# One core, thresholded attention and a maxout feed-forward: the ninth key blocks of a head quad multiplied together in 64x64 tiles, and a new order of work

## The chip, the cores and the metric

The kernel runs on one core of one Trainium2 chip. The metric is the device time of one launch in microseconds (us). Five engines of the core work side by side, each through its own list of instructions in order: TensorE (PE in the profile, with its weight loads as PEld), VectorE (DVE), ScalarE (ACT), GpSimd (POOL), and SyncE (SP), which here only issues DMA transfers. They wait for each other by semaphores.

## The reference, cut to what matters

```
q, k, v: (8, 8, 576, 64) f32     tau = 0.02
scores = (q @ k^T) / 8                       per batch and head, 576 x 576
keep   = scores >= rowmax(scores) - tau      everything else becomes exp(-huge) = 0
attn   = exp(scores - rowmax) * keep;  attn /= rowsum(attn)
x      = attn @ v, heads side by side        (4608, 512)
h      = max(x @ w1, x @ w2, x @ w3)         512 -> 768
out    = h @ w_out                           768 -> 512, f32
```

## The kernel before, in words

**Quads and tiles.** Four heads of one batch make a quad; there are 16. A quad's head number is 2r + i with r and i in 0 and 1. The 576 rows of a head are nine blocks of 64 queries (and nine of 64 keys). A *tile* is 128 query rows against all 576 keys of the heads of one r; a quad has nine chunks of two tiles (r = 0 and 1), so 18 tiles, and the program has 288.

**A tile's way.** `scores` (line 287) multiplies in f32 into one of four slots of PSUM (`bank`, line 179; a slot is two banks of 512 f32 columns). DVE takes the row maximum (`maximum`, line 319). Then the tile goes one of two ways, fixed by a 0 or 1 in the string `MASKED`. Unmasked (0): ACT runs a Prelu that reads PSUM and then an Exp with a row sum. Masked (1): DVE has copied the negated scores out of PSUM together with the maximum, ACT runs one Exp, and DVE does the comparison, the product and the row sum in one instruction (`numerators`, line 339). DVE makes the reciprocals of a chunk, POOL scales both tiles to bf16 (`normalized`, line 351, the tile `P`), and SP issues a transposing DMA (`turned`, line 360) into the quad's `ptq`: nine blocks of 128 keys by 1152 columns. In blocks 0 to 3 lie the first eight key blocks of r = 0, in blocks 5 to 8 those of r = 1, and block 4 holds the ninth key blocks of both: r = 0 on partitions 0 to 63, r = 1 on 64 to 127.

**The product with V.** `product` (line 366), once per quad and r, runs over five blocks m: four with `vb` (V of 128 keys) and the fifth with `vrb`, which is V of the ninth key block padded with zeros on the other r's 64 partitions, so that all 128 rows of block 4 can be multiplied. For each m and each run of columns (512 and 64 wide) two matmuls stand side by side, i = 0 and 1, each 128 rows by 64 columns of the array. In the profile these are `o<-ptq,vb` and `o<-ptq,vr`. The padded tiles `vrs` are made once (line 219) and their zero halves set by six memsets on DVE (line 553); `cast_v` (line 221) fills them with two POOL casts per quad. One product is copied out of its slot by DVE (r = 0), the other by ACT (r = 1), into `xt`. Batch 7 alone is cut into two parts of 256 and 320 query columns, so it has four products per quad of half the width.

**The feed-forward.** `ffn` (line 432) follows a batch behind: 18 hidden pieces `ph` per batch (six column blocks by three weight matrices), of which ACT copies the first and DVE takes the maximum with the others (`hm`, `hT`), and output pieces `po`. A piece is issued in two halves (F and B in the order), each 64 rows by 128 columns of the array, two abreast.

**What sets the order.** Nothing is scheduled by the compiler: `_Ordered` chains each engine's instructions as they are written, and the string `ORDER` says in which order they are written. A letter is one step: S a tile's scores, T a transpose of q or k on PE, O a product, F and B the halves of a feed-forward piece (the digit is the PSUM slot), m the maximum, e the first pass of ACT, n the second one of an unmasked tile, k that of a masked one on DVE, r reciprocals, p one scaling on POOL, q a swap of q's halves, y a cast of V, z a weight cast, t a transposing DMA, l a load, g a weight load, o a store, w and x the copies of a product by DVE and ACT, h and v those of hidden pieces, u those of output pieces. Since each engine takes its letters in order and waits by semaphore, only the order of letters of one engine among themselves acts, and the buffers that they share.

Of the kernel before, what the change touches and what calls it, by code (L numbers as in the profile page):

```python
# [24 lines left out]
010100101001000000011101001010000001100010001000101000011000100000100000  # L25
000011111001100001001001001001000001011100101001000110001010010000010011
000010011101100001001100100001001010001100010111000001000100000110000101
001001001101100000110001000100100100001100100011100111010011010111110110
# [12 lines left out]
lllllmlyelgS2ymylS3emgnlT0mleS1lakS2nlqermS3ylmeS0pmeS1kpS3elmS2nlzmelrmnT1pS0tcnperkT1pameS1zmteS3knpS0rnmp  # L41
emS2permeqS1mnqT3meqktepS0ncS2ntrpmS3npretprmeS1pmnS0tpmS3npmS1etpmeS0rT2mnplkeT1akgeS2qmgepmteS3rkpekntS0pe
rrnmT2pncS3ptamepS1meqtrS2meyqnS3lmqeS0pmelpknT1lpS2nmeymeS3lrkepS0tcnT2rpnmS1tpnmaprrmS0eS2pmteS1pmT3epctep
meT3O0ykntnyS2etrykpnO1wnprmaS0xptrS3meS2zmeS1mzgeS0mlnS3pmleS1pmelO2qmelpkteO0nrnklpS3nlwgxprrmS2leS0pmeF3q
tmT1eBqcF0eqkthBpnS2vS1nF3pmnF0pmBerBkepS2vhT1tnprmS0S3apmetS1zmeS2rmpeF3tmF0epBkepF1tnBvBznvS2ghS3rymnF0gmS
1eplBrkepF2tnmF3BnpvBnqvT1S0hprrcT2S3pamS1eymzF2emBeqgkF0etyS3nS1vpnmtF2pBmezBveS3prgnS0mtS1phrmT3epO2metzeF
0wpnS1gcqS2nmBqnmO3zekepgS1xvlF2nS3mtnF0rrmpBeBlpveS1lphS2mntF3zmeBrpS0evS1lpnmF2lnpS3rmleBptmS1nzvS0nS3mtpn
S2rpeF1rmepmtepS0mBepmtekF3ektekT2uBarklpukS0uqlS2urS1mlnS3pmleO0pmlepmelO2wtnkS1xrS0tepmF2myF3eBkepT1tBhcF0
nqvT2T1laByrcynS3qvS2nlqmF1tnpF0meS3pBelmBlhrrF2kpelS1vnBlprF3mnlS0pveBtprmS1hS2pmeS3tpmeS0pmF2emF1eBkeT3Bva
tF0nvqT2T3BkqlaS1nrcS3phmtS2npmF0epF1mteBqkBeqF3lnvS2lnBrvplS0hmtpS1F3meS2mteBrmepS0vnpO1rekpnO3mtnpweS2yrrt  # L50
xS1mF0yymT3epBcnS1pvS2nptF3meS0pmeBomT2hS1okeF0omF3ntBkaBervS1ponrF2vpemS0ptuS3mpeF2metknT1T3rknBparrceS0puS
3mqtuS1mpeS2mpeS3lmF0peomepS1ketqT3S2ncBqnmlqnmlO3ekluktO1urnwperrS0pxS3mptnS2mS1pempS3etmF0peF2meBlkBelS1kh
oF3nrmlF0pnBtvpBerrvS2phlS1mnpS3tmF0peS2mpeBmeF3vF1eoBkntS0vnBS2rmhpS3mepS1mteyF2mF0eyBkteBnrvT3pF1aovT2ynBp
lrcS3hplS0mnyF2lmF1elBykepBlnvT3tS0aS2vnO3rrmtpnmpeS1weptS2mS0prmO3eqtmeqF1eqlT0S2xqcBnlpmS3hlpS0meF2ymF1elB
knlF3vnBokBetS2hvS0nrrF3mpF1mpeBkBpetF2vnprS0uvnT3ptmS2aS1pmeS0trmF3epmnpkeS2tS0ermpBnmopnkS1uS2rurompS0eF3o
mpelmpeS2lkpeS0lmS1elqBmelqmetkO2unktO0erwpurkpT1txT2cS3apF0nmtT1qS2ceBqmnS1yF3hmF2eyrBpeBvptnF0pS1vnBrmtpS3
hS2pmeS0mtS1eF3meF2meBkBeF0knF1vnBBrvhpS3nvT0pF2akyF1tnBmyS0velByrmlS3phS2rlempF1lmyeF0pklBepS3tnvS2nBrmptO1
meprvepS2wnS3plmF0nF1rmepBlkeqS2lBhmtT3nyS0vnS2mqlO1emtpecT2xT0rS3pacF1eqmF2lnyBklqeT0BvlaS3khoS1qnmF0tF2pme
BrBopnvS3teprvF0pnrmS1puS2meS3prmS0epF1tmepmepT2ktBeqncT3tuS0kaS2urqmS3tnpmS1nF0pmemteS3repS1mS2lepmBelykteS
3kuO1rumplnmlpO0ewterpT2xS1cqnoS3mpF0nF2metBkeBkF1hlF3nvBlnrrS0pvlnBpmS2lhS1ymleF0mtS3epBmepF2vF1etkBnS0vnS3  # L60
rmBnpS2rhmpF0emF1pteBkpBerF3vnS2ptvnT0pBramS1pthS0mepF3meqtT2rBecpS1nvylT0ynS2pmlS3amlS1eomS0elO2rmpeomeplO3
ketnwT1F0nctF2xkBnBrvpS1hrF3pmS0qBemqS2onvF1yeF0mBopkeF3tyBnS2vqhBrlrnmpT1S0vaptS2empF1S3mpelBkeplF0vntS2rum
S1pnS0mtepF3rmepmetqS2kS0epBnmmteS1rkepS2lmuS0ulpmS1nlymT3yetF2cekeT3oBrknpamoS0npS3mnS1qtmuO0qurrmqelO2wpel
kpelS0xS3meptF2mS1peBemytF0hrkT3pBecF2nS1vpnS3rymtBpnmS0epS1vlnF3mF2etBmeBkhF0lkeF3nBrvpS1nrvBpnS2mptS0hmpeS
3meF2tmF1eBkeBlrvnT0plS3ravlpS2nlmqF0nlS1mqeBtrrmpF2eS3phBlmepS0tvepS1mS2npS3mepO0meknO1meownT3orxkT2pS0tacF
1nF2qrmeBtpS3evpBmS0tyhF1meT2yBcqoeF3rpkT2F0aptBnvBnS2pvS1hqtmF3nqT0meBrS1npvF2npmT3BactS1ervF3prmS0pueS2omp
F3ekqelmT1ntS0qcnBpmekteS2S1urrmpF0uompekS3eptS2nmS1pnmlO3ermtpekO2pnwS1ykxtyS3emS2BomeyrmepS1rukpS2uoF3meF0
opmnBtykBhpS1ervS2eptmO3pO0mxnS3txS2rmepF0empF1ekBtBevF3hkS2nS0mnBrmF1npF2vepBkBtS0hvO3emO2xkS1xerS3rpmF2mpF
0eF1kpteBnBvpF3BvtBrhkpF2S0vS1prmBptmF3eF0pveBtBhS1vS2mS3mF0F1mBkBF2vhF3keBeO0vnO1kF2kxeBwurS1rvpS0mpS2F3mpe
tmpeS0eoF1mnketBknkBurrupoF2puF0hptF3uvF2pvF1hF0tvF3rvpF2hF1vopF0vF3thF2vF1vF0hoF3vF2ovF1hF0vF3vO2uoO1wF0xF3  # L70
F2hF1vF3vF2hF1vF3vF2hF1vF3vF2hF1vF3vF2hF1vF3vF2hF1vBvF3uuooBF2uuuooo
# [31 lines left out]
def kernel(  # L103
# [262 lines left out]
    def product(L, r, target, part=None):  # L366
# [19 lines left out]

        def on_vector():
            ps = st["ps"]
            dst = target(L["b"])[:, 2 * L["qd"] + r, :]
            if part is None:  # L390
                vector.tensor_copy(out=dst, in_=ps[:, 0:S])
            else:
                vector.tensor_copy(out=dst[:, 256:S], in_=ps[:, 0:320])

        def on_scalar():
# [6 lines left out]
            else:  # L402
                scalar.activation(out=dst[:, 256:S], in_=ps[:, 0:320], func=AF.Copy)
        p = _Piece((L["b"], L["qd"], r, part), first)
        p.vector = on_vector if part != 1 and r == 0 else None
        p.scalar = on_scalar if part == 1 or r == 1 else None
        return p
# [188 lines left out]
    line = {k: [] for k in "menkrptahvuxwcq"}  # L596
# [6 lines left out]
    def issue(what, where):  # L603
# [149 lines left out]
```

## Time and profile before

| | us |
|---|---|
| median of 3 runs | 447.69 (447.66 to 450.87) |
| profiled execution: span from first to last instruction | 445.0 |
| what lies around the span (median less span) | 2.7 |
| PE busy | 423.6 |
| ACT busy | 394.4 |
| DVE busy | 393.2 |
| POOL busy | 315.9 |

The profiled execution has no time of its own beside its span; the median of the runs is 2.7 us longer, and those 2.7 us are taken as what lies around the span. "Busy" is a union of spans of instructions, and a matmul's span in the profile is longer than the time for which it holds the array (their starts are closer together than their ends), so a busy PE can still have short holes; start times of neighbouring matmuls tell more.

### The profile page before, as it was taken

How to read it: one execution, taken by the hardware profiler on the slowest of the kernel's cores; microseconds unless marked ns; L12 is line 12 of the kernel's file. 1: busy time of each engine (PE TensorE's matmuls, PEld its weight loads, DVE VectorE, ACT ScalarE, POOL GpSimd, SP SyncE). 2: the span in 40 equal slices, each digit the busy share in tenths (PEclk: the TensorE clock that was granted, in tenths of full speed). 3: DMA queues.
4: the chain of work that ended last, by engine and by line, in shares of the span. 5: the costliest groups of instructions: out<-in, count | busy, mean ns of one | idle time of the engine just before them, and what ended most of it. 6: DMA issues, size and time to landing. Idle time of an engine off the chain costs nothing.

```text
span 445.0 us, 14089 instructions
## 1 busy us (share of the span) xinstructions
PE 423.6 (95%) x5193; PEld 313.3 (70%) x5193; DVE 393.2 (88%) x1093; ACT 394.4 (89%) x804; POOL 315.9 (71%) x422
## 2 busy tenths in 40 slices
PE   7767799999999999999999999999999999999995
PEld 5434557767787767777687867867687778777772
DVE  4989889999999999989989998999999999989641
ACT  4999999999999999999998999999999999956422
POOL 3998989989686686686768885859767789562300
PEclk9998899999999999999999999999999999999999
DMA  8989999999999978999797999899999979882902
GB/s 251 331 162 213 243 195 234 221 245 229 215 255 195 250 165 175 234 187 228 179 223 170 200 224 182 211 234 199 197 220 202 253 121 173 148 122 34 217 13 108
DMA packets 212773, 87.44 MB, mean 196 GB/s; under 512 B 185824, under 2 KB 199648, under 8 KB 212704
## 3 DMA queue, kind: packets, MB, share of 16 engines
q1 hardware_dynamic: 212000, 85.69, 93.6%
q10 hardware_dynamic: 704, 0.85, 0.6%
q8 instruction: 41, 0.67, 0.6%
q14 instruction: 28, 0.23, 0.2%
HBM read 34.60 MB, written 9.44 MB: 99 GB/s over the span
## 4 chain that ended last, share of the span: by engine, by line
PE 81%; ACT 7%; DVE 6%; issue 4%; POOL 2%; DMA 1%; DVEq 0%; POOLq 0%; ACTq 0%
PE ph L91 30%; PE sc L91 28%; PE po L91 11%; PE o L91 8%; ACT z L91 6%; PE tp L91 4%; DVE z L91 2%; DVE unused L91 2%; DMA qm<-in_q_dram 1%; POOL P L91 1%; DVE hm L91 0%; POOL w L91 0%; ACT qt L91 0%; POOL qs L91 0%; DVE hT L91 0%
## 5 line engine op out<-in xcount | busy, mean ns | idle before, releaser
L91 POOL TENSOR_SCALAR P<-z,rs 128x576 bf16<-128x576 f32 x288 | 228.1, 807 | 85.7 <-DVE rs L91 36.4
L91 PE MATMUL sc<-kt,qt 64*128 64x320 f32 (+2 forms) x640 | 179.1, 429 | 4.9 <-ACT z L91 4.4
L91 PE MATMUL sc<-kt,qs 64*128 64x256 f32 (+2 forms) x640 | 178.6, 418 | 4.7 <-ACT z L91 2.7
L91 PE MATMUL ph<-xt,w 64*128 64x288 bf16 (+2 forms) x2160 | 163.9, 283 | 0.3
L91 PEld LDWEIGHTS <-w 64*128 64x128 bf16 (+1 forms) x2160 | 124.8, 94 | 30.9 <-issue 5.3
L91 DVE TENSOR_SCALAR_CACHE_REDUCE unused<-sc 128x576 bf16<-128x576 f32 x183 | 133.2, 749 | 8.9 <-PE sc L91 8.4
L91 ACT ACTIVATE z<-sc,nm 128x576 f32<-128x576 f32 x183 | 131.3, 740 | 8.5 <-DVE unused L91 5.2
L91 ACT ACTIVATE z<-z 128x576 f32<-128x576 f32 x183 | 123.5, 680 | 0.1
L91 PEld LDWEIGHTS sc<-kt,qs 64*128 64x128 f32 (+1 forms) x640 | 92.4, 178 | 25.3 <-ACT z L91 8.1
L91 PEld LDWEIGHTS sc<-kt,qt 64*128 64x128 f32 (+1 forms) x640 | 92.4, 178 | 19.8 <-ACT z L91 9.3
L91 DVE SCALAR_TENSOR_TENSOR z<-z 128x576 f32<-128x576 f32 x105 | 84.1, 811 | 0.4 <-ACT z L91 0.4
L91 DVE TENSOR_SCALAR_CACHE_REDUCE z<-sc 128x576 f32<-128x576 f32 x105 | 77.7, 752 | 7.4 <-PE sc L91 3.4
L91 ACT ACTIVATE z<-z,nm 128x576 f32<-128x576 f32 x105 | 79.1, 773 | 3.6 <-DVE z L91 3.2
L91 POOL COPY qs<-qt 64x640 f32<-64x640 f32 (+3 forms) x68 | 47.0, 692 | 14.4 <-ACT qt L91 11.0
L91 PE MATMUL po<-wo,hT 64*128 64x512 bf16 (+1 forms) x480 | 54.0, 356 | 0.1
L91 DVE TENSOR_TENSOR hm<-ph,hm 128x576 bf16<-128x576 f32 (+2 forms) x54 | 37.0, 686 | 13.0 <-PE ph L91 11.8
L91 ACT ACTIVATE hm<-ph 128x576 bf16<-128x576 f32 (+2 forms) x54 | 32.1, 594 | 18.4 <-PE ph L91 18.1
L91 PEld LDWEIGHTS <-hT 64*128 64x128 bf16 (+1 forms) x480 | 29.6, 97 | 17.1 <-issue 2.9
L91 DVE TENSOR_TENSOR hT<-ph,hm 128x576 bf16<-128x576 f32 (+2 forms) x54 | 37.2, 688 | 3.1 <-PE ph L91 0.6
L91 PE MATMUL o<-ptq,vb 128*64 128x64 bf16 (+2 forms) x544 | 38.7, 282 | 0.0
L91 ACT ACTIVATION_READ_ACCUMULATOR z<-z 128x1 f32 x183 | 36.2, 198 | 0.0
L91 PEld LDWEIGHTS <-vb 128*64 128x64 bf16 x544 | 22.6, 111 | 15.1 <-issue 6.8
(32 smaller groups left out, 274.2 us busy)
## 6 DMA issues: line engine op xcount, KB each, us to landing
vm<-in_v_dram SPq DMA_DIRECT2D x32, 256.0 KB, 5.1
out_dram<-ob SPq DMA_DIRECT2D x31, 256.0 KB, 2.8
qm<-in_q_dram SPq DMA_DIRECT2D x15, 512.0 KB, 4.5
km<-in_k_dram SPq DMA_DIRECT2D x15, 512.0 KB, 5.4
stage<-in_moe_w_dram SPq DMA_DIRECT2D x9, 512.0 KB, 5.3
ptq<-P SPq DMA_TRANSPOSE x144, 4.1
stage<-in_moe_w_out_dram SPq DMA_DIRECT2D x3, 512.0 KB, 4.7
qm<-in_q_dram SPq DMA_DIRECT2D x16, 64.0 KB, 2.9
```

Source lines behind the costliest of these rows:

```text
L91: ins = fn(*a, **kw)
```

## The change

Four things change.

1. `vrb` is a tile of 128 keys by two heads and no zeros: partitions 0 to 63 hold V of the ninth key block for r = 0, partitions 64 to 127 for r = 1. One cast on POOL fills it; the three padded tiles, their memsets and the second cast go.
2. A product runs over four blocks only and leaves its sums open. A new step N, after both products of a quad (and part), issues the ninth key blocks of both: for each run of columns four matmuls of 64 rows by 64 columns, r = 0 on the upper rows of the array and r = 1 on the lower, each r into its own slot. Only then are both products copied out (w and x).
3. In the second part of batch 7 the columns of the product stand at 256 to 575 of the slot, where they stood at 0 to 319.
4. `MASKED` has 114 ones in place of 105, and `ORDER` is another string: the same steps, with 18 N more and 16 y fewer, in another order on every engine.

```
-    vrs = [one.tile([128, 4, D], BF16, name=f"vr{x}") for x in range(3)]
...
-        L["vrb"] = vrs[(2 * L["b"] + L["qd"]) % 3]
-        for r in range(2):
-            rows = slice(64 * r, 64 * r + 64)
-            pool.tensor_copy(out=L["vrb"][rows, 2 * r:2 * r + 2], in_=L["vr"][rows])
-            yield
+        L["vrb"] = vp.tile([128, 2, D], BF16, name="vrb")
+        pool.tensor_copy(out=L["vrb"], in_=L["vr"])
+        yield
...
-                2: ((256, 896, 0, 256), (512, 576, 256, 64))}[part]
-
-        order = [(m, run) for m in range(5) for run in runs] if part is None else \
-            [(m, run) for run in runs for m in range(5)]
+                2: ((256, 896, 256, 256), (512, 576, 512, 64))}[part]
+
+        order = [(m, run) for m in range(4) for run in runs] if part is None else \
+            [(m, run) for run in runs for m in range(4)]
 
         def first(where):
             st["ps"] = ps = bank("o", where)
             for m, (*q0, p0, n) in order:
                 for i in range(2):
-                    w = vb[:, 2 * r + i, (1, 3, 0, 2)[m], :] if m < 4 else vrb[:, 2 * r + i, :]
-                    tensor.matmul(ps[64 * i:64 * i + 64, p0:p0 + n], w,
-                                  pt[:, 4 if m == 4 else m + 5 * r, q0[i]:q0[i] + n],
-                                  start=(m == 0), stop=(m == 4))
+                    tensor.matmul(ps[64 * i:64 * i + 64, p0:p0 + n], vb[:, 2 * r + i, (1, 3, 0, 2)[m], :],
+                                  pt[:, m + 5 * r, q0[i]:q0[i] + n], start=(m == 0), stop=False)
+
+        def ninths(run):
+            *q0, p0, n = run
+            rows = slice(64 * r, 64 * r + 64)
+            for i in range(2):
+                tensor.matmul(st["ps"][64 * i:64 * i + 64, p0:p0 + n], vrb[rows, i, :],
+                              pt[rows, 4, q0[i]:q0[i] + n], start=False, stop=True)
...
-    for t in vrs:
-        for x in range(2):
-            vector.memset(t[64 - 64 * x:128 - 64 * x, 2 * x:2 * x + 2, :], 0.0)
...
             p.first(where)
-            for k, fn in (("x", p.scalar), ("w", p.vector)):
-                if fn:
-                    line[k].append(fn)
+            line["N"].append(p)
+        elif what == "N":
+            both = [line["N"].pop(0) for _ in range(2)]
+            for run in both[0].runs:
+                for p in both:
+                    p.ninths(run)
+            for p in both:
+                for k, fn in (("x", p.scalar), ("w", p.vector)):
+                    if fn:
+                        line[k].append(fn)
```

The order at three places. PE, quad 0 (batch 0), around its products with V. Before, the first product ends with its own ninth block (`vr`), a tile's scores follow, and then the second product begins:

```order
L91 LDWEIGHTS vr_100
L91 MATMUL o<-ptq,vr_100 64x64
L91 MATMUL sc<-kt,qt 128x256
L91 MATMUL sc<-kt,qs 128x320
L91 LDWEIGHTS vb
L91 MATMUL o<-ptq,vb 64x512
```

In the changed program PE goes at this quad from the last block of the second product straight to the ninths:

```order
L91 MATMUL o<-ptq,vb 64x64
L91 LDWEIGHTS vb
L91 MATMUL o<-ptq,vb 64x64
L91 LDWEIGHTS vrb
L91 MATMUL o<-ptq,vrb 64x512
```

and leaves them with scores:

```order
L91 LDWEIGHTS vrb
L91 MATMUL o<-ptq,vrb 64x64
L91 MATMUL sc<-kt,qt 128x320
L91 MATMUL sc<-kt,qs 128x256
L91 MATMUL sc<-kt,qt 128x256
```

What moved: the ninth blocks of both products stand behind both, eight matmuls in a row, and the scores no longer stand between the products.

PE, quad 1, from the end of its products to the first hidden piece of the feed-forward (`ph`, with the weights `w_63`). Before:

```order
L91 LDWEIGHTS vr_101
L91 MATMUL o<-ptq,vr_101 64x64
L91 MATMUL sc<-kt,qs 128x256
L91 MATMUL sc<-kt,qt 128x320
L91 MATMUL sc<-kt,qs 128x320
L91 MATMUL sc<-kt,qt 128x256 x2
L91 MATMUL sc<-kt,qs 128x320
L91 LDWEIGHTS w_63
L91 MATMUL ph<-xt,w_63 128x288
```

Now:

```order
L91 LDWEIGHTS vrb
L91 MATMUL o<-ptq,vrb 64x64
L91 MATMUL sc<-kt,qs 128x320
L91 MATMUL sc<-kt,qt 128x256
L91 LDWEIGHTS w_63
L91 MATMUL ph<-xt,w_63 128x288
```

What moved: three tiles' scores stood between the products and the first hidden piece, and one stands there now; 48 tiles' scores stood ahead of quad 1's products, and 49 do now, so the first hidden piece comes after 50 tiles in place of 51.

ACT, around its copy of quad 1's second product (`xt<-o`). Rows with `z<-sc,nm` are the first pass of unmasked tiles, `z<-z,nm` that of masked ones, `z,sm<-z` the second pass of unmasked ones. Before:

```order
L91 ACTIVATE z<-z,nm 128x576
L91 ACTIVATE z<-sc,nm 128x576 x2
L91 ACTIVATE z,sm<-z 128x576 x3
L91 ACTIVATE xt<-o 128x576
L91 ACTIVATE z<-sc,nm 128x576
```

Now:

```order
L91 ACTIVATE z<-z,nm 128x576
L91 ACTIVATE z<-sc,nm 128x576
L91 ACTIVATE z<-z,nm 128x576
L91 ACTIVATE xt<-o 128x576
L91 ACTIVATE z<-sc,nm 128x576
```

What moved: six passes of tiles stand directly ahead of the copy before, three of them second passes; now the second passes stand behind it.

More of the change, by code (lines that the diff above doesn't have):

```diff
@@ L24 @@
 MASKED = """
[L25 to L28, printed above, removed]
+001110001000100001011000011010010001001000101101001001000000100000011000
+001010100111100001001001000100010001011100101001100010001010010000111000
+110010100101010010011100000001001011000110100110111001000100001110000101
+001010001101110001100001000100100100001100001101010110110101000111111111
 """
@@ L46 @@
[L46 to L65, printed above, removed]
@@ new lines @@
+hS1S2emS0zlpgtpF3F1qemmettkeBqvBS2rnnzF0T3mtBvpnhpkS2meraeF1S0BS3mgevmF2nprS1mepypqBpnF0S3lvkBegF2F1BmhrvS0z
+tneBpplzF3nnS2mvBeS1T0mrtT2mhS3pncgpgaS2F0mtBererlmpekvS1emF3S2nntS0pBlemeS1ppzqtS2mvmrF3qentT0pBF1rcmS0pppz
+nhenBS3mvO2rmgO1NekglentexnS0F3S1klwmmrnF2plpqypeeBzpBvS0hS1tmF3S2mBtrF1pzpneemrS0vBlneS3mvnS2mrppyS0mnemF1k
+S2eS3mreptnepBepmS0F3kpmrS2uutS1kenmnT0arBpekS2emtupueS0mkptpqqO1lltO3emNrlelpkwS2tllxltrlS0F3myF1lmBnpeekph
+T2cBF0T3T2vnanqpBS1cvqmF3S2BmneF0hrS1pyperBkF3S2mnBrvmvF0enS1BtS2plmmloppeS3hS0eS1emmtpmF3eekF2BBleF0tlT1vnt
@@ new lines @@
+rBvT3aT2haS1pS0kF2crtS3nmBnpmtmF0eS1tqpeeqvBptlmrppF2nveS3lntBmrlF0hS1kpyeBS2mpnvmrenpqyplS3O1qtO0mrNepexkT2
+nS3wF0cS1mrBpmnenS2S1oF3vF0pBtmmeS1pekhlS2toF3rBmmeptynevlT1aBprS2vS0nmmeF1ukketepF3kS1mT2T0rrcBS1ptpqnnaoup
+umS0eppmrS2S3mmeeeS0F1eS2qnkpkmT3BS0rnceunrmkmueppS3tlltemO2epO1NotllltS0krwpxS3ppqyF2qnpnmS1BmeS3hF0emmeeF2
+BnS1BkrvmnrF3loS0BvpleyyrS2mnpmpphS1ppF0etmS3emllBeF1nF2BtevkrpS0BvS3nS1hmmtleS2lmmetF3tkF0eBpleT1BvrvanT2nF
+3cS1BnmF0S2BrhkF3mpeT1vnrBpprveaS0S2nmT1S3pqpncmpS0meeeqmeS1tO2pqmtotlloeO3ltqNF0S1klwBxrpkppS2mrhmF3S0epBmF
@@ new lines @@
+2nenS1pvBF0mF3nleBBtottvkS2hF0keF1rurvpmT3BeapkppyrpvS1S2mnS3S0pnemF1mtS3emkS2rpBenepltS0memkmrutpuS2neS3emF
+1rmpqkynpS2pqeBemS0uuS2O3kmemekO1NeS0rwT2xoF1olppnT3mnT0BcS2aS3rncqhF0qtF1pBtemmpBkevrF2eS3vlmpnBptnlS0S1S3h
+ermmempS2F0ypmF1BBelrteoevnF3T2F0akkqvBBS2nhkymF1pqpnF3verBBS0rvtpmhnS2S1F3mrmlpBpeS0evlmS2eF1pnS3BmnleF2mtl
+lvrlttS0eppptyBmS1ehF3lepT2BmltnS0lnltcS1rkvO2O3tmNpmeprT1nnexrapkwS0pqF3qyemT1T2cpBF0S1anepkBS2hvF3S0mreBF1
+mekmrnvF2qBeS3vS0unpS2tS1omlrmeppqptlmmnF3pktT0BpecS1eekryuT2uaS0mnS3lomtmrtleF2enpS1kpS3qppnemmS0Bmkerppeue
@@ L72 @@
+S3pmF0oeBmrBokettF2peuokoruoF3uhF1pkkF2hvvruF3pF1F2hppF0pvvF3F1vvF2F0F3hvtovhtF1F2F0F3htvF1voF2O0uvO3NvF1xwF
+2hF3F0vF2vhF3F0F2hvF3vvF0F2F3vF0hF2hovF3vF0F2vhF3vvF0vBuuF2BuouoF3uooo
 """
@@ L392, in on_vector @@
             else:
-                vector.tensor_copy(out=dst[:, 256:S], in_=ps[:, 0:320])
+                vector.tensor_copy(out=dst[:, 256:S], in_=ps[:, 256:S])
         def on_scalar():
@@ L402, in on_scalar @@
             else:
-                scalar.activation(out=dst[:, 256:S], in_=ps[:, 0:320], func=AF.Copy)
+                scalar.activation(out=dst[:, 256:S], in_=ps[:, 256:S], func=AF.Copy)
         p = _Piece((L["b"], L["qd"], r, part), first)
@@ L406, in product @@
         p.scalar = on_scalar if part == 1 or r == 1 else None
+        p.runs, p.ninths = runs, ninths
         return p
@@ L595 @@
                 O=products(), F=pieces())
-    line = {k: [] for k in "menkrptahvuxwcq"}
+    line = {k: [] for k in "menkrptahvuxwcqN"}
     casts = iter([w[1] for w in wl])
```

25 lines of the change are left out of this document (14 added, 11 removed).

## The prediction

> **What bounds the kernel now.** I read the page first, its busy times and its forty slices of 11 us.
>
> ```profile
> span 445.0 us, 14089 instructions
> PE 423.6 (95%) x5193; PEld 313.3 (70%) x5193; DVE 393.2 (88%) x1093; ACT 394.4 (89%) x804; POOL 315.9 (71%) x422
> PE   7767799999999999999999999999999999999995
> DVE  4989889999999999989989998999999999989641
> ACT  4999999999999999999998999999999999956422
> ```
>
> Four engines look full on average, so the averages decide nothing. The slices do: PE is at 7 or so in the first five and at 9 from then to the last but one, while ACT is at 9 in just those first slices. So there are two regimes, and I asked for windows cut where they change. Columns: stretch, its length, then busy us of PE, PEld, DVE, ACT, POOL with instruction counts, granted clock, DMA share, GB/s.
>
> ```profile
> 10.00:50.00 40.00, 27.11 (x229) 15.82 (x230) 37.14 (x111) 39.09 (x84) 37.88 (x49) 0.94 1.05 244
> 50.00:67.50 17.50, 16.36 (x166) 10.52 (x166) 14.79 (x44) 16.89 (x35) 14.77 (x21) 0.94 1.09 199
> 67.50:400.00 332.50, 332.01 (x4291) 252.33 (x4290) 313.41 (x865) 315.89 (x642) 252.98 (x333) 1.00 1.01 203
> 430.00:445.00 15.00, 10.53 (x90) 5.98 (x87) 4.36 (x9) 3.57 (x8) 0.00 (x0) 0.99 0.21 80
> ```
>
> From 10 to 50 us ACT is busy 39.09 of 40 and PE 27.11: the start is paced by ACT, with POOL (37.88) and DVE (37.14) just behind. There is no feed-forward work yet, because batch 0 must pass through attention first. From 67.5 to 400 PE is busy 332.01 of 332.5, ACT 315.89 and DVE 313.41: PE bounds this stretch, with 16.6 us (5.0%) left on ACT and 19.1 (5.7%) on DVE. So PE time saved after 67.5 shortens the program nearly in full as long as ACT and DVE stay below PE, and the start gets shorter only by what ACT sheds.
>
> The boundary is the first hidden piece, from the timeline:
>
> ```profile
> 62.55 1.22 PE L91 MATMUL o<-ptq,vb 128*64 128x512 bf16 x15
> 67.54 0.65 PE L91 MATMUL ph<-xt,w 64*128 64x288 bf16 x7
> ```
>
> Quad 1's products begin at 62.55 and the feed-forward at 67.54.
>
> **The change, part by part.** *The ninths.* One quad's two products, whole, in the timeline of PE (start, length, shape, count):
>
> ```profile
> 115.82 0.43 PE L91 MATMUL sc<-kt,qs 64*128 64x320 f32 x1
> 116.18 1.18 PE L91 MATMUL o<-ptq,vb 128*64 128x512 bf16 x16
> 117.19 0.41 PE L91 MATMUL o<-ptq,vr 128*64 128x512 bf16 x4
> 117.44 1.16 PE L91 MATMUL o<-ptq,vb 128*64 128x512 bf16 x16
> 118.43 0.41 PE L91 MATMUL o<-ptq,vr 128*64 128x512 bf16 x4
> 118.78 0.53 PE L91 MATMUL sc<-kt,qt 64*128 64x320 f32 x1
> ```
>
> I go by starts. Four blocks take 117.19 - 116.18 = 1.01 us, the ninth 117.44 - 117.19 = 0.25. A quad pays 0.25 twice. If four 64x64 matmuls run abreast, the same columns stream once for both r, so N takes 0.25 and each quad saves 0.25. The groups by shape count the ninths: 56 matmuls of 512 columns and 64 of 64 (8 of the latter and the 16 of 256 are batch 7's parts):
>
> ```profile
> L91 PE MATMUL o<-ptq,vr 128*64 128x512 bf16 x56 | 11.4, 382 | 0.0
> L91 PE MATMUL o<-ptq,vr 128*64 128x64 bf16 x64 | 6.8, 193 | 0.0
> ```
>
> That is 28 whole products, 14 quads, and batch 7's two quads in parts with the same columns in sum: 16 x 0.25 = **4.0 us** of PE, all of it after quad 0.
>
> Do four run abreast? The fifth chunk of each quad already does its scores in that shape:
>
> ```profile
> 160.91 0.43 PE L91 MATMUL sc<-kt,qt 64*128 64x320 f32 x1
> 161.18 0.43 PE L91 MATMUL sc<-kt,qt 64*128 64x320 f32 x1
> 161.54 0.43 PE L91 MATMUL sc<-kt,qs 64*64 64x256 f32 x2
> 161.56 0.49 PE L91 MATMUL sc<-kt,qt 64*64 64x320 f32 x2
> 162.29 0.44 PE L91 MATMUL sc<-kt,qt 64*64 64x320 f32 x2
> 162.68 0.53 PE L91 MATMUL sc<-kt,qt 64*128 64x320 f32 x1
> ```
>
> Four start within 0.02 us of each other (x2 at 161.54, x2 at 161.56), so yes in f32; in bf16 with sums left open no row shows it.
>
> *The shape switch.* In one shape, a 320-column pass follows the one before by 161.18 - 160.91 = 0.27. From the last 64x128 pass to the first 64x64 one it is 161.54 - 161.18 = 0.36, and back, 162.68 - 162.29 = 0.39 with 0.27 of streaming: a change of the array's shape costs 0.09 to 0.12 us. The Trainium skill ("TensorEngine Tiling (Array Packing)", Key Properties) says that changing the tiling mode, not just the tile, drains TensorE; the trace agrees, with these 0.09 to 0.12 us, and the page has no price of its own. The rule speaks against this change. Each N is another shape than the products ahead of it, so 18 N add 18 switches; against that, before, PE goes to other shapes between a quad's two products at four places (the first piece of order shown above is one), and some pieces elsewhere move. Counted over PE's whole list there are 94 switches before and 103 now: 9 x 0.1 = **+0.9 us**. Bounds: 0 (if a 128x64 to 64x64 switch needs no drain) and 18 x 0.12 = 2.2.
>
> *Nine more masked tiles.* Rows of ACT and DVE in the start:
>
> ```profile
> 53.47 0.74 ACT L91 ACTIVATE z<-sc,nm 128x576 f32<-128x576 f32 x1
> 54.11 0.68 ACT L91 ACTIVATE z<-z 128x576 f32<-128x576 f32 x1
> 54.77 0.67 ACT L91 ACTIVATE z<-z 128x576 f32<-128x576 f32 x1
> 62.39 0.77 ACT L91 ACTIVATE z<-z,nm 128x576 f32<-128x576 f32 x1
> 63.05 1.36 ACT L91 ACTIVATE z<-sc,nm 128x576 f32<-128x576 f32 x2
> 54.76 0.75 DVE L91 SCALAR_TENSOR_TENSOR z<-z 128x576 f32<-128x576 f32 x1
> 55.44 0.08 DVE L91 DVE_READ_ACCUMULATOR z<-z 128x1 f32 x1
> ```
>
> By starts an unmasked tile costs ACT 0.64 + 0.66 (53.47, 54.11, 54.77), a masked one 0.66 (62.39 to 63.05): 0.64 less. DVE pays 55.44 - 54.76 = 0.68 more. Over the program ACT sheds 9 x 0.64 = 5.8 us and DVE takes on 6.1. Six of these tiles lie between the 46th and the 272nd, so ACT goes from 315.9 to some 312 and DVE from 313.4 to some 317.5, against a PE stretch of 332.5 less 2.9: the fuller of the two falls short of PE by 12 us where it was 16.6. Priced at nothing while this cover holds.
>
> *The start.* Of the first 50 tiles 18 are masked and 16 were: 2 x 0.64 = 1.3 us less for ACT, while DVE's 1.4 more fits into its 40 - 37.14 = 2.9 idle us. The first hidden piece also comes after 50 tiles and not 51. The start paces a tile at about 67.5 / 51 = 1.3 us at most, and that tile still takes PE 0.5 us later (0.27 and 0.22 for 320 and 256 columns, twice, shared by two tiles), so up to 0.8 is gained; but the hidden piece needs both copies of quad 1's products, whose work ahead hardly shrinks, so half of it, 0.4. Together **-1.7 us**; bounds -2.5 and +2, since DVE and POOL stand close behind ACT and could take its place.
>
> *POOL, DVE's memsets, SP.* The casts and memsets that go:
>
> ```profile
> L91 POOL CAST vr<-vr 64x128 bf16<-64x128 f32 x32 | 13.1, 411 | 1.2
> L91 DVE MEMSET vr<- 64x64 uint32 x6 | 0.7, 112 | 1.1 <-PEq L734 0.8
> ptq<-P SPq DMA_TRANSPOSE x144, 4.1
> ```
>
> Sixteen casts fewer (0.41 each, the cast of 128 partitions being as wide per partition): 6.6 us off POOL, which has 80 us idle after 67.5: nothing. The memsets lie in the first us, where DVE has no data: nothing. SP's transposes keep their number; loads now stand among them in other places. A quad's last transpose takes 4.1 us to land, and 13 to 23 tiles' scores stand between its own last ones and the products (12 to 22 before) up to batch 6; nothing, or a PE wait of up to 4 us where a load blocks SP's list.
>
> The sum: 445.0 - 4.0 + 0.9 - 1.7 = 440.2 us of span, and with the 2.7 around it 442.9: I say **443.0 us**, 1.0% less than the median of 447.69. A measurement of this kernel can tell about 1% from no change, 443.2 to 452.2.
>
> **The rivals.** *Held slots.* The first product's slot used to be copied while the second ran; now both stay full until N, and only two of four slots can take scores meanwhile. The copies cost:
>
> ```profile
> L91 DVE CAST xt<-o 128x576 bf16<-128x576 f32 x14 | 10.5, 750 | 0.6 <-PE o L91 0.5
> L91 ACT ACTIVATE xt<-o 128x576 bf16<-128x576 f32 x14 | 9.1, 651 | 1.2 <-PE o L91 1.0
> ```
>
> After N, PE has two free slots, about 1 us of scores, and then needs a slot that ACT frees 0.65 or DVE 0.75 us after N. That fits if each copy is at the head of its engine's list; from 0.3 us of older work ahead of it PE waits. Before, 1.2 us of idling in 14 copies shows ACT almost always behind. With one pass (0.66) ahead at 18 places PE loses up to 18 x 0.4 = 7 us, with two, 18 x 1.0 = 18: 450 to 461, **slower**. Against it: the two engines have 2.2 us of products to work off what is queued, with only two slots' input, and at quad 1 the second passes have moved behind the copy. The Trainium skill (the same page, PSUM Bottleneck) warns that tiling speeds up TensorE but not the copies out of PSUM; no row here shows it, since the products were not held so before.
>
> *The cover is gone.* ACT and DVE have 12 us of room in 330, and both serve PE through four slots. If their lists hold up PE in bunches, the 3.1 us that PE saves turn into idling: 445 to 449, no change.
>
> *Not abreast.* If open sums or bf16 keep the row halves from running together, N takes 0.5: the 4.0 goes, the switches stay: 447.
>
> *A better order.* PE idles 4.5 us in the last 15 and 12.9 from 10 to 50; an order that fills a third of that besides: 436 to 440.
>
> **How the numbers follow.** Forecast, 440 to 445.5: 0.55, three fifths of it below 443.2. Better order: 0.08. Cover gone: 0.17. Not abreast: 0.04. Held slots: 0.16. Faster by over 1%: 0.33 + 0.08 = 0.41; within: 0.22 + 0.17 + 0.04 = 0.43; slower: 0.16. Leaving out half of the better orders and the worse half of held slots, the range is 438 to 453.
>
> **What would show it.** N's first start to the next piece's: 0.35 with the switch if right, 0.6 if not abreast. The first hidden piece at about 65.8 us. PE busy in the stretch after it as full as before, with ACT near 94% and DVE near 96%. Held slots would appear as PE or PEld waits for `xt`, in ACT's or DVE's name, right behind each N. The prediction is wrong if the new order makes PE wait for scores' slots in the middle.

## The result, and the profile after

The changed kernel took 444.54 us (median of 4 runs, 443.89 to 445.51), the kernel before, measured beside it, 447.68 (447.25 to 450.87). The ratio is 0.9947 with a 95% interval of 0.9922 to 0.9972: 0.5% faster. That is inside the bound of 1% that the prediction set for "no change", and clear of 1 by its interval. The forecast was 443.0, so 1.5 us too low. The profiled execution has a span of 442.1 us (445.0 before); a second profile of the same kernel had 443.0. The 2.7 us that were taken as what lies around the span are too many: in every run with both a time and a span on record the difference is 1.7 to 1.9 us, so the profiled execution of the kernel before took some 446.8 us, less than the median. The difference of two times doesn't depend on this.

The page of the changed kernel, its head and the slices of 11 us for three engines:

```profile
span 442.1 us, 14065 instructions
PE 421.6 (95%) x5193; PEld 306.2 (69%) x5193; DVE 401.2 (91%) x1105; ACT 388.1 (88%) x786; POOL 320.7 (73%) x406
PE   7777799999999999999999999999999999999995
DVE  2989999999999999999999999999999999999641
ACT  4998999999999999998999999999999999875422
```

PE lost 2.0 us of busy time, ACT 6.3, and DVE gained 8.0. The picture is the same: five slices in which PE is mostly at 7, then PE at 9. The windows of the changed kernel (stretch, length, then busy us of PE, PEld, DVE, ACT and POOL with counts, granted clock, DMA share, GB/s):

```profile
10.00:50.00 40.00, 29.35 (x236) 16.80 (x232) 37.76 (x108) 38.64 (x80) 35.73 (x47) 0.91 1.11 259
50.00:67.50 17.50, 16.10 (x162) 9.94 (x163) 16.73 (x49) 17.05 (x35) 17.21 (x20) 0.90 0.91 171
67.50:400.00 332.50, 331.15 (x4334) 246.94 (x4335) 321.47 (x888) 312.79 (x634) 255.78 (x323) 1.00 1.03 204
```

The long stretch is bound by PE as before (331.15 of 332.5). DVE, not ACT, is now the fuller helper, at 321.5 (97%), where 317.5 was forecast. PE waits for the slots of scores hardly more than before: between 67.5 and 400 us PE and its weight loads waited 7.4 us for ACT or DVE to free one, 6.5 before, so the sign by which the prediction wanted to be found wrong did not come. In the start PE's granted clock was lower, 0.91 and 0.90 where it was 0.94 in both stretches.

One quad's products, whole, in PE's timeline (start, length, shape, count):

```profile
115.75 0.43 PE L91 MATMUL sc<-kt,qs 64*128 64x320 f32 x1
116.10 2.17 PE L91 MATMUL o<-ptq,vb 128*64 128x512 bf16 x32
118.20 0.44 PE L91 MATMUL o<-ptq,vrb 64*64 64x512 bf16 x8
118.57 0.53 PE L91 MATMUL sc<-kt,qt 64*128 64x320 f32 x1
```

From 116.10 to 118.57 the quad takes 2.47 us; before, from 116.18 to 118.78, it took 2.60, so 0.13 are saved: 0.25 less streaming, and one change of shape more. The step N holds 118.57 - 118.20 = 0.37: 0.25 of streaming and one change of shape. All eight ninth blocks stand in 0.44 us, so four of 64x64 do run abreast in bf16 with open sums.

The start did not get shorter. The same view around quad 1's products and the first hidden piece (in brackets what PE waited for):

```profile
63.53 2.24 PE L91 MATMUL o<-ptq,vb 128*64 128x512 bf16 x32
65.69 0.44 PE L91 MATMUL o<-ptq,vrb 64*64 64x512 bf16 x8
66.92 0.42 PE L91 MATMUL ph<-xt,w 64*128 64x288 bf16 x4
67.59 0.42 PE L91 MATMUL ph<-xt,w 64*128 64x288 bf16 x4 [0.25 <-DVE xt L91]
```

The products begin at 63.53 where they began at 62.55, and the first hidden piece at 66.92 instead of 67.54, with a hole right behind its first matmuls. Set side by side, the DVE passes that finish the hidden blocks start as follows in the two profiles: the first (73.1 us before) 1.1 us later than before, the third (84) 0.2 earlier, the twenty-fourth (257) 0.1 earlier, the forty-second (407) 3.0 earlier, and from there to the end the distance stays. By this measure, what was gained was gained in the second half.

### The profile page after: what moved, and what is told of

Read it like the earlier page. It is cut to its first block, busy times and chain, and to the rows that moved or that the text cites. A ratio compares the mean times of both kernels' runs of the same rounds, so it can differ in the third digit from the quotient of the medians.

```text
span 442.1 us, 14065 instructions
## 1 busy us (share of the span) xinstructions
PE 421.6 (95%) x5193; PEld 306.2 (69%) x5193; DVE 401.2 (91%) x1105; ACT 388.1 (88%) x786; POOL 320.7 (73%) x406
## 4 chain that ended last, share of the span: by engine, by line
PE 72%; DVE 6%; ACT 4%; POOL 2%; issue 2%; DMA 1%; SPq 0%; POOLq 0%; DVEq 0%
PE ph L91 29%; PE sc L91 25%; PE po L91 9%; PE o L91 6%; ACT z L91 4%; PE tp L91 3%; DVE z L91 2%; DVE unused L91 2%; POOL P L91 1%; POOL qs L91 1%; DVE kt L91 1%; DMA out_dram<-ob 1%; POOL vb L91 0%; DVE xt L91 0%; DVE hT L91 0%
## 5 line engine op out<-in xcount | busy, mean ns | idle before, releaser
L91 POOL TENSOR_SCALAR P<-z,rs 128x576 bf16<-128x576 f32 x288 | 236.2, 834 | 75.2 <-DVE rs L91 21.8
L91 PE MATMUL sc<-kt,qt 64*128 64x320 f32 (+2 forms) x640 | 183.5, 431 | 4.7 <-ACT z L91 2.6
L91 PE MATMUL ph<-xt,w 64*128 64x288 bf16 (+2 forms) x2160 | 170.7, 283 | 0.4 <-DVE xt L91 0.2
L91 DVE TENSOR_SCALAR_CACHE_REDUCE unused<-sc 128x576 bf16<-128x576 f32 x174 | 128.1, 749 | 4.6 <-PE sc L91 3.6
L91 ACT ACTIVATE z<-sc,nm 128x576 f32<-128x576 f32 x174 | 125.3, 740 | 5.3 <-DVE unused L91 2.9
L91 ACT ACTIVATE z<-z 128x576 f32<-128x576 f32 x174 | 117.7, 681 | 0.2
L91 DVE SCALAR_TENSOR_TENSOR z<-z 128x576 f32<-128x576 f32 x114 | 95.2, 845 | 0.3
L91 ACT ACTIVATE z<-z,nm 128x576 f32<-128x576 f32 x114 | 86.8, 773 | 4.8 <-DVE z L91 4.5
L91 DVE TENSOR_SCALAR_CACHE_REDUCE z<-sc 128x576 f32<-128x576 f32 x114 | 84.7, 751 | 6.9 <-PE sc L91 3.4
L91 PE MATMUL o<-ptq,vb 128*64 128x64 bf16 (+2 forms) x544 | 35.3, 281 | 0.1
```

Source lines behind the costliest of these rows:

```text
L91: ins = fn(*a, **kw)
```

## The experiments

The ratios are to the kernel before, measured on the same chip, with 95% intervals.

### The changed kernel again

> The changed kernel once more, beside the others on one chip, as the measure for them. Every theory expects 0.995 of before (0.992 to 0.997) and a span near 442.

Measured: 0.9964 (0.995 to 0.9977), 444.75 us. The gain is there again. Its profile has a span of 443.0 and its first hidden piece at 67.44, against 442.1 and 66.92: two profiles of one kernel differ by 0.5 us in the start, and no smaller shift there means anything. Their granted clocks differ too (0.91 and 0.87 from 10 to 50 us).

### The new order and masks, without the ninths' own step

The changed kernel's order, in which the two products of a quad stay where they are, with the padded tiles, two casts and five blocks per product of the kernel before (and its columns for batch 7). The lines show it against the changed kernel, shortened:

```
-        L["vrb"] = vp.tile([128, 2, D], BF16, name="vrb")
-        pool.tensor_copy(out=L["vrb"], in_=L["vr"])
+        L["vrb"] = vrs[(2 * L["b"] + L["qd"]) % 3]
+        for r in range(2): ...
-        order = [(m, run) for m in range(4) for run in runs] if part is None else \
+        order = [(m, run) for m in range(5) for run in runs] if part is None else \
```

> The new order and masks, but each product takes its own padded ninth block again and no step N. Theory 'ninths' (the gain is PE time saved by the ninths): 16 x 0.25 = 4.0 us of streaming come back and 18 shape switches of 0.1 go, so 2.2 us longer than the changed kernel, span 444.3, ratio to before 0.998 to 1.000. Theory 'order' (the gain comes from the order and the masks): as fast as the changed kernel, 0.995.

Measured: 1.0031 (1.0019 to 1.0044). The two ratios split the change in two. The ninths, with the casts and memsets that go with them, are worth 0.9964 / 1.0031 = 0.9933, that is 0.67% or **3.0 us** (the ends of the two intervals allow 1.9 to 4.2). The new order with its 114 masks, alone, costs 0.31% or **1.4 us**.

The sum of the prediction must be split in the same way before it is set beside these. PE's list in this run has 86 changes of shape, against 94 before and 103 in the changed kernel: the ninths add 17, and the new order takes 8 away. At 0.1 us each the sum holds -4.0 + 1.7 = -2.3 us for the ninths and -1.7 - 0.8 = -2.5 us for order and masks. The expectation above has 2.2 for the ninths, by the same count. Where in the program the loss lies isn't read from this run's profile: it is of the slowest of its eight executions (span 447.1, median 446.0), and its granted clock from 50 to 67.5 us was 0.80.

### The old order with the ninths in 64x64

The kernel before, order and masks included, with N put in behind each quad's second product; the two products of a quad were moved together, which moves work of PE from between them at four quads (0, 2, 6 and 8).

> The order and the 105 masks of before, with the ninth blocks of a quad multiplied together (at four quads the two products are brought next to each other). Theory 'ninths': 4.0 us less streaming and some 10 more switches, so 3.0 us off before, span 442, ratio 0.993 to 0.995. Theory 'order': 0.999 to 1.001. Theory 'held slots': the copies come later than this order was made for, so PE waits for slots behind each N and the ratio is over 1.000.

Measured: 1.0398 (1.038 to 1.0415), span 461.6. The arithmetic that saves 3 us in the new order costs 16 in this one. By the trace 3.0, 3.1 and 5.3 of them are lost at three of the four quads whose products were moved (2, 6 and 8), where ACT came to its copy 2.2 to 3.6 us after the ninths. Who idled ahead of the copies, and who waited for them, from the view of the tile `xt` (us, times):

```profile
  PE o L91: 22.0, 19
  PEld sc L91: 11.3, 16
  PE sc L91: 5.4, 8
```

The copies sat 22.0 us until the products were there (3.9 before), and PE with its weight loads then waited 16.7 us for the copies to free slots, where it waited 1.4. This is the rival "held slots" of the prediction at full size, though here the moved products are mixed into it.

### The same with less disturbance

Here these four quads keep their products apart, each with ninths of its own (a step M in place of N), and only the others are pairs. The lines of the order are seen from the kernel before, the code from the changed one.

```
-meT3O0ykntnyS2etrykpnO1wnprmaS0xptrS3meS2z
+meT3O0MykntnyS2etrkpnO1MwnprmaS0xptrS3meS2z
...
-        elif what == "N":
-            both = [line["N"].pop(0) for _ in range(2)]
+        elif what in "NM":
+            both = [line["N"].pop(0) for _ in range(2 if what == "N" else 1)]
```

> The order and masks of before with nothing moved on PE but the ninths: together at the 14 places where a quad's products stand next to each other, each product's own behind it (two 64x64 matmuls, no padding) at the four places where they stand apart. In the earlier run with the old order the trace lost 3.0, 3.1 and 5.3 us just at three of those four places. Theory 'copies too early': at the 14 places DVE and ACT still come to the copies before N is done, with nothing else to do; 14 x (0.25 - 0.1) = 2 us gained and about 7 lost, ratio 1.008 to 1.015. Theory 'moved products' (the loss was only at the moved ones): 0.995 to 0.997.

Measured: 1.0132 (1.0109 to 1.0156), span 451.3. The same view:

```profile
  PE o L91: 12.3, 18
  PEld sc L91: 6.9, 11
  PE sc L91: 2.5, 4
```

Idle copies and a lag that grows in small steps from quad to quad spoke for copies that stand too early in DVE's and ACT's lists. The next run is made for this reading.

### The same, with DVE's copy one pass later

Relative to the run of pairs, step w moves behind the next pass on DVE at ten of the fourteen places where products stand together (and some slot numbers are exchanged so that scores find a free slot):

```
-S1pmelO2qmelpkteO0NnrnklpS3nlwgxprrmS2leS0pmeF3q
+S1pmelO2qmelpkteO0NnrnklpS3nlgxprrmwS2leS0pmeF3q
```

> The kernel before with both products of a quad next to each other, as in the run of pairs (ratio 1.013, copies idle until the product is there 12.3 us), but at these places DVE's copy of its product stands one pass later in DVE's list. Theory 'copies stand too early' (both copies now wait for the end of the second product, and the passes behind them that would free score slots wait with them): the idle time ahead of copies shrinks to 5 to 9 us and the ratio to 1.003 to 1.010. Rival 'slots held' (two slots stay full through two products, wherever the copies stand): ratio 1.011 to 1.018, and PE or PEld waits for the copy in place of what it waited for.

Measured: 1.0255 (1.023 to 1.0281), span 456.5. The view of `xt`, then PE at quad 1's ninths and behind them, with DVE's copy:

```profile
  PE o L91: 5.9, 11
  PEld sc L91: 6.8, 11
  PE sc L91: 5.1, 7
```

```profile
64.47 0.44 PE L91 MATMUL o<-ptq,vrb 64*64 64x512 bf16 x8
65.22 0.43 PE L91 MATMUL sc<-kt,qt 64*128 64x320 f32 x1
66.75 0.75 DVE L91 CAST xt<-o 128x576 bf16<-128x576 f32 x1
67.65 0.50 PE L91 MATMUL sc<-kt,qs 64*128 64x320 f32 x1 [2.00 <-DVE xt L91]
```

The idle time ahead of the copies halved, as the theory said, and the kernel became 5.2 us longer. The two profiles, compared at ACT's passes one by one, show where. At five of the ten places DVE now came to its copy 1.0 to 2.1 us after the ninths (here 66.75, where the ninths end at 64.91), and 6.4 us were lost there (the start had come out 0.6 shorter). At the other five it still came within 0.3 us of them, with 0.3 us of idling in place of 4.2, and only 0.6 us were won. So a copy that stands waiting costs little, and one that comes late costs a good deal: the theory "too early" falls by the second five, while the first five went past the mark and test it no further. The rival's sign is right (PE's waits for copies rose from 9.4 to 11.9 us), its ceiling of 1.018 was too low. Over the four orders these waits and the spans go together: 1.4 us before, 9.4 in the pairs, 11.9 here, 16.7 in the run ahead, with spans of 445.0, 451.3, 456.5 and 461.6, and 1.6 us in the changed kernel.

The strings `ORDER` show what else differs. In the changed kernel, at 16 of the 18 N, two or three pieces of PE into the two free slots stand between N and the first piece that needs a slot of the products (the first N reads `NS1eknxrwS0nmeS2`, with the products in slots 3 and 2). In the old order with ninths there are two at four N, one at eight and none at six. PE runs out of slots behind N where these pieces are missing, unless the copies come at once. That is read from the lists beside PE's waits; no run changed these pieces alone.

### The old start in front of the new rest

About the first 64 tiles in the order and with the masks of before, the rest as changed.

```
-mmlS2eS3mmleS1mkllnyT0eS3nS2T1alglermpceS0emT1S3knmaqrpkS1elmqpS2r
+lllllmlyelgS2ymlS3emgnlT0mleS1lakS2nlqermS3ylmeS0pmeS1kpS3elmS2nlz
```

> Ninths together; the order and masks of before up to the 60th tile's scores (into the first hidden pieces), then the new order and masks. In the changed kernel the first hT is finished 1.1 us later than before. Theory 'start' (that 1.1 us lengthens the program): 1.1 us off the changed kernel, span 441, ratio 0.992. Theory 'absorbed' (by the third hT, at 84 us, the lag is gone): as the changed kernel, 0.995.

Measured: 1.0000 (0.9985 to 1.0015). The start itself is like the changed kernel's (the first hidden block 0.3 us earlier, the second 0.6 later). Then 2.4 us are lost between 84 and 92 us, just behind the splice, and kept to the end. Neither theory expected that; the run says more of splices than of starts, and whether the new start is worth anything stays open.

### The ninths one product after the other

```
-            for run in both[0].runs:
-                for p in both:
+            for p in both:
+                for run in p.runs:
                     p.ninths(run)
```

> The changed kernel, with N issued product by product (512 and 64 columns of r = 0, then 512 and 64 of r = 1) in place of both products' 512 first. Theory 'in order' (a matmul that waits for its tile holds up those behind it, so the two row halves overlap only in part): N takes 0.43 to 0.5 in place of 0.25, 3 to 4 us longer than the changed kernel, ratio 1.003 to 1.005. Theory 'free': PE fills the other row half anyway, ratio as the changed kernel, 0.996.

Measured: 0.9948 (0.9931 to 0.9966), as fast as the changed kernel. In the list of PE r = 0 now has both of its column runs ahead of r = 1: 512, 512, 64, 64, then again 512, 512, 64, 64. Its timeline cut to 119.6 to 119.7 us, and then whole:

```profile
119.67 0.42 PE L91 MATMUL o<-ptq,vrb 64*64 64x512 bf16 x4
```

```profile
119.67 0.45 PE L91 MATMUL o<-ptq,vrb 64*64 64x512 bf16 x8
120.05 0.53 PE L91 MATMUL sc<-kt,qt 64*128 64x320 f32 x1
```

N still takes 120.05 - 119.67 = 0.38, and four matmuls start at 119.67, the other four at 119.91 or just after. By their records the first four are the 512s of both products, so the 512s of r = 1 started ahead of the 64s of r = 0 that stand before them in the list. The saving doesn't hang on the interleaved order in which the change writes them.

### Two casts of the start placed later

One of `z` and one of `y` on POOL move some tiles back, behind the first quad's products.

```
-rpklmerpzapS0pmtryptS3me
+rpklmerpapS0pmtrptS3me
```

> The changed kernel with two POOL casts of 1.03 us each (a weight block and the V of quad 2, neither needed before the feed-forward or quad 2) moved behind the scalings of quad 1. Theory 'POOL paces the start' (POOL is busy 17.21 of 17.5 us from 50 to 67.5): quad 1's products and the first hidden piece come 1 to 2 us earlier, ratio 0.992 to 0.994. Theory 'ACT or DVE pace it': no change, 0.996.

Measured: 0.9953 (0.9934 to 0.9971), span 443.4, first hidden piece at 67.73. No change: these casts don't pace the start.

### Eight masks fewer, eight masks more

Both keep the changed kernel's order; for eight tiles the second pass changes engine at its place (`k` on DVE to `n` on ACT, or back). Fewer (106):

```
-pneaS1rtmS3S2pemeS3pqemkmpgneS0rk
+pneaS1rtmS3S2pemeS3pqemnmpgneS0rk
```

> The changed kernel with eight tiles unmasked again (106 ones), each second pass at the same place but on ACT: ACT 8 x 0.64 = 5.1 us more, DVE 5.4 less. Theory 'cover' (both stay below PE): no change, 0.995 to 0.998. Theory 'balance' (the nine masks are part of the gain): 1 to 3 us longer, 0.999 to 1.003.

Measured: 1.0112 (1.009 to 1.0135), span 449.8. More (122), at eight other tiles close to those:

```
-pneaS1rtmS3S2pemeS3pqemkmpgneS0rk
+pkeaS1rtmS3S2pemeS3pqemkmpgneS0rk
```

> The changed kernel with eight more masked tiles (122), the opposite of the run with 106: their second pass stands at the same place of the written order, but on DVE in place of ACT. ACT sheds some 8 x 0.64 = 5.1 us, DVE takes on 8 x 0.68 = 5.4 us. Taking eight masks away cost 7.7 us of span. Theory 'balance' (ACT is what PE waits for in bunches, so each mask more relieves it): faster than the changed kernel, ratio to the kernel before 0.985 to 0.993. Theory 'fitted order' (the order of work is fitted to one set of masks, and eight tiles whose work stands on another engine make PE wait whichever way they go): slower, ratio 1.000 to 1.012, with PE's waits for copies of products (xt) at several places and in DVE's name.

Measured: 1.0039 (1.0025 to 1.0053), span 446.3. The long stretch of 106, and of 122:

```profile
67.50:400.00 332.50, 325.11 (x4228) 243.09 (x4226) 312.77 (x862) 312.72 (x637) 250.37 (x318) 1.00 1.00 199
```

```profile
67.50:400.00 332.50, 329.55 (x4272) 244.87 (x4271) 322.47 (x890) 307.62 (x617) 255.70 (x320) 1.00 1.02 201
```

With 106 masks DVE and ACT are balanced to a tenth of a us, both with 20 us of room, and that is the slowest of the three. Both ways lose against 114 (7.7 and 4.2 us of span against the changed kernel's first profile, 6.8 and 3.3 against its second), in steps of some 0.3 to 1.7 us at a handful of places. PE's waits of weight loads for score slots, by who freed them (us, times, longest), in the changed kernel, with 106 and with 122:

```profile
PEld sc L91 <- ACT z L91: 10.9, 26, 2.0
PEld sc L91 <- DVE z L91: 6.0, 14, 1.0
```

```profile
PEld sc L91 <- ACT z L91: 14.1, 27, 2.0
PEld sc L91 <- DVE z L91: 5.5, 12, 1.0
```

```profile
PEld sc L91 <- ACT z L91: 10.8, 26, 1.6
PEld sc L91 <- DVE z L91: 8.6, 17, 1.4
```

Whichever engine got the work, PE waited more for it (3.2 us for ACT, 2.6 for DVE) and for the other hardly less. These waits are a part of what was lost, not all. "Fitted order" holds in its sign and size (1.000 to 1.012 expected) and "balance" falls; but the waits are for scores' slots, while those for the copies, which I had named for 122, stayed at 1.6 us. The copies themselves sat idle 15.8 us with 106 masks, 6.4 with 122 and 5.8 without an edit, again without PE waiting for them. For how far the order is fitted to these 114 there are two neighbours, no more.

### What paces the start

Two kernels, with one run each, leave out half of one pass in the first 40 tiles: ACT's second pass of the unmasked ones, or DVE's pass of the masked ones.

```
+            some = number[g, idx] < 20
+            zn = zn[:, 0:S // 2] if some else zn
-            scalar.activation(out=zn, in_=zn, func=AF.Exp, scale=-1.0 / FLAT, accum_out=acc)
+            scalar.activation(out=zn, in_=zn, func=AF.Exp, scale=0.0 if some else -1.0 / FLAT, accum_out=acc)
```

```
+            some = number[g, idx] < 20
+            zn = zn[:, 0:S // 2] if some else zn
-            vector.scalar_tensor_tensor(out=zn, in0=zn, scalar=thr, in1=zn,
+            vector.scalar_tensor_tensor(out=zn, in0=zn, scalar=0.0 if some else thr, in1=zn,
```

> The changed kernel with half of one pass left out in the start: for the unmasked among the first 40 tiles, ACT's second pass runs over 288 of the 576 keys with a constant exponent, so the row sums and half of the numerators of these tiles are not the reference's. Some 25 passes shorter by about 0.29 us: 7 us off ACT before 55 us. Theory 'ACT paces the start', as predicted: the first hidden piece, at 66.9 and 67.4 in the two profiles of the changed kernel, comes 3 to 6 us earlier, and the span falls by as much (437 to 440). Theory 'the start is paced by a ring of engines that each wait for another one, or by DVE': 0 to 1.5 us earlier.

> The changed kernel with half of one pass left out in the start: for the masked among the first 40 tiles, DVE's instruction for comparison, product and row sum runs over 288 of the 576 keys with a threshold of nought, so the row sums and half of the numerators of these tiles are not the reference's. Some 15 passes shorter by about 0.34 us: 5 us off DVE before 55 us. Theory 'ACT paces the start': the first hidden piece comes 0 to 1 us earlier than 66.9 to 67.4 us. Theory 'DVE paces it': 2.5 to 5 us earlier.

In the view of groups by line between 10 and 60 us (count, busy us, mean ns, idle before and its releasers) and in PE's timeline, the changed kernel's second profile, for comparison:

```profile
L91 POOL TENSOR_SCALAR P<-z,rs 128x576 bf16<-128x576 f32 x36 | 29.5, 832 | 5.2 <-DVE rs L91 2.2 <-issue 1.5 <-ACT z L91 0.9
L91 ACT ACTIVATE z<-z 128x576 f32<-128x576 f32 x26 | 17.6, 681 | 0.1
L91 DVE SCALAR_TENSOR_TENSOR z<-z 128x576 f32<-128x576 f32 x14 | 13.8, 986 | 0.0
67.44 0.42 PE L91 MATMUL ph<-xt,w 64*128 64x288 bf16 x4
```

ACT relieved:

```profile
L91 ACT ACTIVATE z<-z 128x288 f32<-128x288 f32 (+1 forms) x27 | 11.9, 444 | 0.1
67.16 0.42 PE L91 MATMUL ph<-xt,w 64*128 64x288 bf16 x4
```

DVE relieved:

```profile
L91 POOL TENSOR_SCALAR P<-z,rs 128x576 bf16<-128x576 f32 x41 | 30.7, 760 | 4.2 <-DVE rs L91 2.0 <-ACT z L91 1.3
L91 DVE SCALAR_TENSOR_TENSOR z<-z 128x288 f32<-128x288 f32 x14 | 9.3, 668 | 0.9 <-ACT z L91 0.9
60.94 0.38 PE L91 MATMUL o<-ptq,vb 128*64 128x512 bf16 x1
62.12 2.14 PE L91 MATMUL o<-ptq,vb 128*64 128x512 bf16 x31 [0.80 <-DMA ptq<-P]
65.41 0.67 PE L91 MATMUL ph<-xt,w 64*128 64x288 bf16 x8
```

ACT shed 5.7 us, and the first hidden piece came 0.3 us earlier (67.44 to 67.16) with the span unchanged (443.0 to 442.9): "ACT paces" falls in the changed kernel. DVE shed 4.5 us, and the piece came 2.0 us earlier, the span 2.4 (440.6). Against the changed kernel's first profile (66.92 and 442.1) both are 1.5. That is the sign of "DVE paces", below its 2.5 to 5. In between, the row maxima of the 32nd to 40th tiles came 3 to 4 us earlier; half of that was lost again at quad 1's products, where PE waited for the transposing DMA of `ptq` (the row at 62.12). Relieving DVE also made each scaling on POOL shorter, 832 to 760 ns, though POOL's work was the same. Each is one profile, and the kernel before was not tried in this way. The granted clock from 10 to 50 us differs as well, 0.87 in the profile compared with, 0.91 with ACT relieved and 0.96 with DVE relieved, and what it has in the 2.0 us wasn't separated.

## Why the prediction came near and was wrong in its parts

**The ninths, -4.0, and the shape switches: right.** N took 0.37 where I had named 0.35, and "Not abreast" falls. Against the same order without them they are worth 3.0 us. The sum's 4.0 - 0.9 = 3.1 is next to that by luck, since its 9 switches are those that the ninths add less those that the new order takes away; on the same footing it had 2.3. The 0.13 us of one quad, 16 times, are 2.1. Whether the other 0.7 to 0.9 us are the casts that went, or only the width of the intervals, isn't known.

**The start, -1.7: this step failed.** Order and masks together came to +1.4 us where the sum, with the 8 switches that the order takes away, had -2.5. I took the engine with the highest share in the start, ACT at 39.09 of 40, for its pace, and let DVE's extra 1.4 us vanish in its 2.9 idle ones. In the changed kernel ACT's relief did nothing; DVE's did. And DVE's extra was mis-sized. These are the masked second passes between 10 and 60 us, before and changed:

```profile
L91 DVE SCALAR_TENSOR_TENSOR z<-z 128x576 f32<-128x576 f32 x13 | 11.6, 900 | 0.4 <-ACT z L91 0.4
L91 DVE SCALAR_TENSOR_TENSOR z<-z 128x576 f32<-128x576 f32 x14 | 14.2, 1013 | 0.0
```

I had priced one at 0.68 by the starts in a single row. In the start they take 0.90 and 1.01 us on average, so DVE's extra there is 14.2 - 11.6 = 2.6 us, nearly all of the idle time that I had counted on. The first hidden block was finished 1.1 and 1.6 us later than before in the two profiles, so the case of the bound of +2 ("DVE and POOL stand close behind ACT and could take its place") is the one that came; whether ACT paced the start of the kernel before stays open, and so does the part of the lower clock.

**Nine more masks, nothing while the cover holds: not shown, and the argument was wrong.** Twelve us of room on the average of 330 say nothing of a place. Moving eight passes from one engine to the other cost 3 to 8 us with room on both (10 us and more). What the nine masks of the change cost by themselves wasn't run; they are part of the +1.4.

**POOL, memsets, SP: nothing, as far as is seen.** The casts of the ninth blocks fell from 13.1 to 5.6 us, but POOL's busy time rose from 315.9 to 320.7, mainly since each scaling became longer (mean 807 ns before, 834 now, 288 times).

**Held slots: a real mechanism, rightly described.** In the old order it came as the rival said and inside its 450 to 461 or just above, 453 to 464 us. In the changed kernel PE waits 1.6 us for copies in all. The rival gave PE two free slots, some 1 us of scores, before it needs a slot of the products. The new order has two pieces or more for them behind 16 of its 18 N, the old one with N put in behind four; that this is why the new order escapes is read from the lists and wasn't tested by itself. The copies themselves are as long as before (medians of 0.75 us on DVE and 0.65 on ACT). The Trainium skill ("TensorEngine Tiling (Array Packing)", PSUM Bottleneck) warns that tiling speeds up TensorE but not the copies out of PSUM; these medians agree.

**Cover gone, better order.** The first put the result at 445 to 449 by a bunching of ACT and DVE behind N, and the time is next to its range; the runs place the missing gain in order and masks and not behind N, where PE hardly waits. The second didn't come.

So 443.0 against 444.5 has a sound half, the streaming on the engine that bounds the program, and an unsound one, what a new order is worth. That it came within 1.5 us is in part luck: the ninths gave 0.7 us more than their share of the sum, order and masks 3.9 less. The whole span fell by 2.9 and 2.0 us in two profiles where 4.8 was forecast.

## What to carry to other kernels

Columns that need not be streamed on the bounding engine are counted by the starts of neighbouring matmuls, and that count, less the changes of shape, held to 0.02 us for a quad (0.13 saved, 0.25 - 0.10 counted). Before a run that leaves out one part is set beside a term of a sum, the term is counted against the same run. What a rearranged order gains or loses is not read from the averages of the engines that serve it: an engine at 97% of a window may not set its pace, and one with 20 us of room may still be late at several places. A change that holds buffers longer, and the order that makes room for it, are one change: either of them alone was slower here than neither. A place to look is the list of the engine that needs the buffers: how much it has to do in the free ones before it needs a held one.

## What the runs showed of the hardware

**DVE's masked pass and POOL's work hold each other up.** Four rows of the changed kernel's timeline, two of DVE and two of POOL at the same moments:

```profile
33.17 1.65 DVE L91 SCALAR_TENSOR_TENSOR z<-z 128x576 f32<-128x576 f32 x1
44.20 0.74 DVE L91 SCALAR_TENSOR_TENSOR z<-z 128x576 f32<-128x576 f32 x1
```

```profile
33.17 1.03 POOL L91 CAST vb<-vm 128x1024 bf16<-128x1024 f32 x1
44.20 1.21 POOL L91 COPY qs<-qt 64x512 f32<-64x512 f32 x1
```

At 33.17 DVE's pass takes 1.65 us, a little less than POOL's 1.03 and its own 0.75 after each other; at 44.20 DVE takes 0.74 and POOL the longer 1.21, where such a copy takes 0.75 on average. Over the program, DVE's masked pass takes 752 ns on average where POOL is idle beside it (28 of them) and 880 where POOL works for over 0.4 of it (77), and the row maximum, which reads its tile from PSUM, 752 and 749. POOL's scaling takes 747 ns without such a pass beside it and 1.1 us where one overlaps half of it. The Trainium skill ("SBUF — State Buffer", Who interferes with whom) states just this: a DVE instruction with two SBUF inputs contends with a GpSimd instruction that reads SBUF, and issue order decides who is blocked. These rows agree. In this kernel it makes a mask dearer where POOL is busiest, and in the start POOL is busy 34 to 38 of 40 us; that the start's pace comes from it, and not from DVE's own 0.75 us, wasn't separated.

**Matmuls of different row halves don't keep the order of the list.** The run of the ninths in turn had four 512-column matmuls start together at 119.67 with two 64-column ones between them in the list. The Trainium skill ("TensorE: Matmul & The Clock Gate", Part 3: Packing small matmuls — row/col tiling) says that matmuls are strictly first in, first out in start and end; in this trace the starts were not (the ends of matmuls are modelled in the profile and say nothing). The 0.38 us of N are too short for it as well: in list order r = 1's 512 columns would have begun only with the 64s of r = 0, 0.24 us later by these starts, and N would have taken about 0.6, by this estimate.
